# An attention and SwiGLU kernel: the first output tile turned earlier, output products ahead of the last down groups, and other PSUM banks for the first segment's values

## The chip, the cores and the metric

The kernel runs on one core of one Trainium2 chip. The metric is the device time of one execution in microseconds; lower is better. The kernel before has a median of 1744.81 us over three runs (1742.91 to 1745.12).

## The reference

The input x has 2048 rows of D = 576. Two branches are computed from it and mixed row by row with a gate g. Branch a is attention with H = 32 heads of 18 in four segments of 512 rows: softmax inside the segment, and a running memory of the segments before. Branch b is a SwiGLU of width F = 4608. Cut to what matters here:

```python
g = sigmoid((x * gate_w).sum(-1, keepdims=True))
for s in range(4):                                 # segments of 512 rows
    p = softmax(qs @ ks.T * scale + mask)
    o = sig(beta) * (phi(qs) @ M) / (phi(qs) @ z) + (1 - sig(beta)) * (p @ vs)
    M, z = M + phi(ks).T @ vs, z + phi(ks).sum()
a = concat(o) @ wo
b = (silu(x @ w_gate) * (x @ w_up)) @ w_down
out = g * a + (1 - g) * b
```

## The kernel before

The program is one list of instructions, written out by hand in the order in which each engine is to run them; every engine takes its own part of the list strictly in order and waits on semaphores where the data needs it. Products are made exact by splitting both operands into a high and a low part: the high part is made by ScalarE (`split`, L128), the low part by VectorE (L129), and 14 matmuls (`products`, L151) make one product over the 576 rows.

**Projections.** Segment by segment (s = 0 to 3), nine chains make queries and keys (`qk`), then eight value steps (`v_step`, L375) make the values: four blocks of 128 rows for each of two column halves. Every chain and step takes one of TensorE's eight result banks (PSUM) from a cyclic list. Six chains of the first segment use `first_tile`, which cycles through banks 0 to 4 after three chains that hold 0, 1 and 2; so the chains come to stand in banks 0, 1, 2, 3, 4, 0, 1, 2, 3. The value steps take theirs from `v_tile` (L108): 5, 6, 7, 3, 4, 5, 6, 7 in the first segment, then 5, 6, 7 in turn. The next segment's chains use `chain_tile`, banks 0, 1, 2. A bank is free again when ScalarE and VectorE have read the last result out of it. During the first segment's value steps the two engines also split the next segment's x (`x_split`: four tiles xo at L128 and L129, the last one xs at L162 and L163), which the next segment's first chain needs.

**Gate/up units and down groups.** Then 72 units (L1006; two halves of 36, each with its own 1024 rows) make gate and up by seven products apiece (`seven`, L998 and L1001), in three banks: a, y and xx. ScalarE copies and applies silu (L1055 to L1074), VectorE adds and multiplies (L1062 to L1080); the results `sg0` and `sg1` are split into `hh` and `hl` for the down product. After each product a `tick()` runs what `defer(k, ...)` put k ticks ahead. After every third unit 16 down groups are due (`down_group`, L851: nine matmuls over three units, 320 or 256 columns; VectorE adds the result to `ya`, L856), in the next unit's ticks. The attention itself runs in the same ticks. When it is done, `c_open` opens the buffers of the output pass and defers the loads of wo in six chunks (`wo_load`, L888; high part L891, low part L892; chunks 1 to 3 make `wos[0]`, 4 to 6 `wos[1]`) and of the first tiles.

**The output pass** (from L1112) takes 16 tiles of 128 rows. `c_load(n)` fetches a tile of the attention's result (`o`, L897) and, for segments 1 to 3, its memory part (`me`, L901); `f_load(n)` fetches the down result (L908). `c_tr` (L911) adds the two on GpSimd (L913), copies the last 64 columns (L914), turns the tile on TensorE (four matmuls with the identity at L917, one at L919) and splits it (`oh`, `ol`, `os`). One step later the tile is multiplied by `wos[0]` and `wos[1]`, mixed with the gate on VectorE (L1129, L1130) and stored by SyncE (L1133). The last unit leaves 16 down groups behind; the steps of the output pass run them between their own matmuls: `downs(4)` in step 0, `downs(2)` behind each later turn and `downs(1)` behind each half product, as long as there are any. Group 0 is the first that needs hh and hl of the last unit.

Of the kernel before, what the change touches and what calls it, by code (L numbers as in the profile page):

```python
# [65 lines left out]
def gated_mix(ctx, tc, xT, xrest, wf, wfr, wfh, wd, wv, wo, beta, cmask, ident, bmask, out):  # L66
# [32 lines left out]
    def banks(*ids):  # L99
        turn = cycle(ids)  # L100
        return lambda shape=(P, L): ps.tile(list(shape), F32, name=f"bank{next(turn)}")
# [3 lines left out]
    pair_tile = banks(3, 4)  # L105
    first_tile = banks(0, 1, 2, 3, 4)
    lone_tile = banks(7)
    v_tile = banks(5, 6, 7, 3, 4, 5, 6, 7, *8 * (5, 6, 7))  # L108
    a_tile = banks(0)
    x_tile = banks(1)  # L110
    y_tile = banks(2)
# [15 lines left out]
    def split(hi, lo, src):  # L127
        nc.scalar.activation(hi, src, AF.Copy)  # L128
        nc.vector.tensor_sub(lo, src, f32(hi))  # L129
# [31 lines left out]
    def xs_split(xs, raw):  # L161
        nc.scalar.activation(xs, raw, AF.Copy)  # L162
        nc.vector.tensor_sub(xs[64:128], raw[64:128], f32(xs[64:128]))  # L163
# [81 lines left out]
    def r_fetch(f):  # L245
        nc.sync.dma_start(f32(rhs[f % 2][:96]).rearrange("p j n -> p (j n)"), rc[f // 4, :, f % 4])
# [437 lines left out]
    with ExitStack() as st:  # L684
# [12 lines left out]
        def row_tile():  # L697
            return rw.tile([P, L], F32, name="row")

        def w_fetch(f):  # L700
            ops = wops[1, f] = [None] * 7

            def one(j):
                ops[j] = op_tile()
                nc.sync.dma_start(f32(ops[j]).rearrange("p a k n -> p (a k n)"), wc[f, j])

            return [(j + 2 if f else FIRST[j], lambda j=j: one(j)) for j in range(7)]
# [153 lines left out]
        wos, tiles = [], {}  # L861
# [49 lines left out]
        def c_tr(o, me):  # L911
            if me is not None:
                nc.gpsimd.tensor_add(o[:, 0:D], o[:, 0:D], me)  # L913
            nc.gpsimd.tensor_copy(o[:, 576:640], o[:, 512:576])  # L914
            ta = half_tile([P, 4, P])
            for k in range(4):
                nc.tensor.transpose(ta[:, k], o[:, P * k:P * k + P], idt)  # L917
            tb = lone_tile([P, P])
            nc.tensor.transpose(tb, o[:, 512:640], idt)  # L919
            oh = cps[0].tile([P, 4, P], F32R, name="oh")  # L920
            ol = cps[0].tile([P, 4, P], F32R, name="ol")
            os_ = cps[0].tile([P, P], F32R, name="os")
            split(oh, ol, ta)
            xs_split(os_, tb)
            r = []
            for k in range(4):
                r += [oh[:, k], ol[:, k], oh[:, k]]
            return r + [os_, os_]
# [30 lines left out]
        def feed(half, f):  # L959
            return [(f // CH, i, hf, hs, ds, yas[half], half) for i in range(8) for hf in range(2)]  # L960
# [32 lines left out]
        def seven(t, j, first=True):  # L993
# [6 lines left out]
                    n += 1  # L1000
            nc.tensor.matmul(t, rem[:, RPOS[j]], XR[j], start=False, stop=True, skip_group_check=True)  # L1001

        draw = {}
        for o, fn in start:
            defer(o - 7, fn)
        for pos, (half, f) in enumerate(seq):  # L1006
            if f == 0:
                yas[half] = yp.tile([P, 8, D], F32, name="ya")
            q = f % CH
            nxt = seq[pos + 1] if pos + 1 < len(seq) else None  # L1010
            if q == 0 and f:
                groups += feed(half, f - 1)
            plan = []
            if nxt:
                plan += w_fetch(nxt[1]) if nxt[0] and nxt[1] < KEPT else w_make(*nxt)
                if nxt != (0, 1):
                    plan.append((1 if nxt[1] else 10, lambda f=nxt[1]: r_fetch(f)))
                for n, h in enumerate(BLOCKS.get(pos, ())):
                    plan += r_block(h, 4 * n)
                if f + 2 < FT:  # L1020
                    wraw_of[f + 2] = [None, None]
                    for u in range(2):
                        plan.append(((2, 5)[u] if f or not half else 5 + u, lambda u=u, f=f: wraw_of[f + 2].__setitem__(u, w_load(f + 2, u))))
            if pos == FT - 2:
                X2, XR2 = [[None, None] for _ in range(7)], [None] * 7
                plan += [(o + 8, fn) for o, fn in x_second(X2, XR2)]
            for o, fn in plan:
                defer(o + 1, fn)
            step = [0]

            def tick():
                k = step[0]
                step[0] += 1
                if k == 0:
                    while stores:
                        nc.sync.dma_start(*stores.pop(0))
                if half == 0:
                    if (q, k) in ((0, 3), (1, 3), (2, 2)):
                        draw[f] = d_load(f)
                    if (q, k) in ((1, 1), (1, 7), (2, 4)):  # L1040
                        g = f - 1 if k == 1 else f
                        ds[half, g] = d_split(g, draw.pop(g))
                elif (q, k) in ((1, 0), (1, 2), (2, 1)):
                    g = f - 1 if k == 0 else f
                    ds[half, g] = d_fetch(g)
                beat(k, half)

            ops, rem = wops.pop((half, f)), rhs[f % 2]
            hh = fp.tile([P, 2, L], F32R, name="hh")
            hl = fp.tile([P, 2, L], F32R, name="hl")  # L1050
            hs[half, f] = hh, hl
            a, y, xx = a_tile(), y_tile(), x_tile()
            p5, sg0, sg1 = (row_tile() for _ in range(3))
            seven(a, 0)
            nc.scalar.activation(xx, a, AF.Copy)  # L1055
            tick()
            seven(y, 1)
            nc.scalar.activation(p5, y, AF.Copy)
            tick()
            seven(a, 2, False)  # L1060
            y = y_tile()
            nc.vector.tensor_add(y, a, p5)  # L1062
            tick()
            seven(xx, 3, False)
            nc.scalar.activation(sg0, xx, AF.Copy)  # L1065
            tick()
            seven(a, 4, False)
            xx = x_tile()
            nc.scalar.activation(xx, a, AF.Copy)  # L1069
            nc.vector.tensor_add(p5, a, p5)  # L1070
            tick()
            nc.scalar.activation(sg0, sg0, AF.Silu)  # L1072
            seven(y, 5, False)
            nc.scalar.activation(sg1, y, AF.Silu)  # L1074
            exp_table()
            tick()
            tick()
            seven(xx, 6, False)
            nc.vector.tensor_mul(sg0, xx, sg0)
            nc.vector.tensor_mul(sg1, p5, sg1)  # L1080
            if q == CH - 1:
                defer(2, lambda t=(hh[:, 0], hl[:, 0], sg0): split(*t))
            else:
                split_by(2, hh[:, 0], hl[:, 0], sg0)
            split_by(3, hh[:, 1], hl[:, 1], sg1)
            tick()
            assert not groups
            if f == FT - 1:
                groups += feed(half, f)
                if half == 0:  # L1090
                    for n in range(BREAK):
                        beat(None if n > 1 else n)
                    XO, XR = X2, XR2
                    assert not groups
# [13 lines left out]
        def downs(k):  # L1108
            for _ in range(min(k, len(groups))):
                down_group(*groups.pop(0))  # L1110

        ffs = {n: f_load(n) for n in range(2)}  # L1112
        for n in range(17):
            if n < 16:
                if n + 2 < 16:
                    tiles[n + 2] = c_load(n + 2)
                    ffs[n + 2] = f_load(n + 2)
                nxt = c_tr(*tiles.pop(n))
                downs(2 if n else 4)
            if n:  # L1120
                tt = order[n - 1]
                ff = ffs.pop(n - 1)
                for hf in range(2):
                    c = slice(288 * hf, 288 * hf + 288)
                    t = chain_tile()
                    products(t[:, :288], ops, w_mov(wos[hf], 288))
                    downs(1)
                    if hf == 0:
                        nc.vector.tensor_scalar_mul(ff, ff, g1[:, tt:tt + 1])  # L1129
                    nc.vector.scalar_tensor_tensor(ff[:, c], t[:, :288], gg[:, tt:tt + 1], ff[:, c],  # L1130
                                                   op0=OP.mult, op1=OP.add)
                    if hf == 0 and sent:
                        nc.sync.dma_start(*sent.pop(0))  # L1133
                    if n == 16:
                        nc.sync.dma_start(out[0, P * tt:P * tt + P, c], ff[:, c])
                if n < 16:
                    sent.append((out[0, P * tt:P * tt + P, :], ff))
            ops = nxt
# [54 lines left out]
```

## Time and profile before

| | |
|---|---|
| median of three runs | 1744.81 us (1742.91 to 1745.12) |
| the profiled execution | 1747.73 us |
| its span, first to last instruction | 1746.0 us |
| mean granted TensorE clock | 0.998 |
| TensorE busy (matmuls) | 1715.8 us, 98% of the span |
| weight loads, beside the matmuls | 1483.9 us, 85% |
| VectorE, ScalarE, GpSimd busy | 1368.6, 1093.6, 936.3 us |
| DMA queue 1 | 325.83 MB, 76.6% of 16 engines |

A row of the timeline gives the start in us, the time that the piece took, engine, line, operation, output<-input and, in brackets, how long the engine had been idle before it and what ended that. Matmuls overlap, so the spacing of starts tells more than the time of one. PE is TensorE and PEld its weight loads, DVE is VectorE, ACT ScalarE, POOL GpSimd, SPq SyncE's queue of DMA issues.

### The profile page before, as it was taken

The numbers are of one execution on the slowest core, as the hardware profiler recorded it, in microseconds if no ns is written. First come the engines' busy times: TensorE is split into PE (matmuls) and PEld (weight loads), VectorE is DVE, ScalarE is ACT, GpSimd is POOL, SyncE is SP. The second block draws the span as 40 slices with busy tenths as digits, with TensorE's granted clock in tenths as the row PEclk, the third lists the DMA queues.
The fourth block names the chain that finished last, engine by engine and source line by source line (L and its number), as shares of the span: only waits on it lengthen the run. The fifth ranks groups of instructions, "written<-read, shape, count | busy, mean of one in ns | idle before, by whom it ended". The sixth has DMA issues, their size and how long they took to land.

```text
span 1746.0 us, 34931 instructions
## 1 busy us (share of the span) xinstructions
PE 1715.8 (98%) x11868; PEld 1483.9 (85%) x11868; DVE 1368.6 (78%) x3231; ACT 1093.6 (63%) x2198; POOL 936.3 (54%) x1194
## 2 busy tenths in 40 slices
PE   9999999999999999999999999999999999999999
PEld 7899978878888888887887788888888888888799
DVE  6567587989898889898989677787888777887655
ACT  7666575765676577667656755665666576656511
POOL 4434645656665656665666555555555555555221
PEclk9999999999999999999999999999999999999999
DMA  7654499998998888897979976777687668866544
GB/s 263 237 190 154 149 307 179 213 221 180 225 216 206 175 207 199 187 199 192 209 146 287 263 176 132 188 168 157 156 185 173 155 149 186 169 129 147 168 134 139
DMA packets 524003, 328.06 MB, mean 188 GB/s; under 512 B 411184, under 2 KB 460336, under 8 KB 523824
## 3 DMA queue, kind: packets, MB, share of 16 engines
q1 hardware_dynamic: 523824, 325.83, 76.6%
q8 instruction: 93, 1.52, 0.4%
q14 instruction: 86, 0.70, 0.1%
HBM read 165.76 MB, written 76.09 MB: 139 GB/s over the span
## 4 chain that ended last, share of the span: by engine, by line
PE 78%; ACT 8%; DVE 4%; DMA 3%; issue 3%; POOL 2%; SPq 1%; DVEq 0%; ACTq 0%; POOLq 0%
PE bank L998 29%; PE bank L851 25%; PE bank L151 10%; PE bank L1001 5%; PE bank L720 3%; PE bank L768 2%; ACT L1072 1%; PE bank L769 1%; ACT L991 1%; DMA pt<-p 1%; ACT pe L738 1%; PE bank L406 1%; POOL ws L256 1%; DVE hl L941 1%; PE bank L342 1%
## 5 line engine op out<-in xcount | busy, mean ns | idle before, releaser
L753 POOL TENSOR_TENSOR p<-pe,p 128x512 f16<-128x512 f32 x320 | 374.4, 1170 | 457.7 <-DVE p L752 438.2
L851 PE MATMUL bank<-dw,hh 128*128 128x320 f32 (+1 forms) x2304 | 491.2, 306 | 4.1 <-ACT hh L128 2.8
L851 PEld LDWEIGHTS bank<-dw,hh 128*128 128x128 f32 x2304 | 383.3, 191 | 15.6 <-ACT hh L128 3.1
L738 ACT ACTIVATE pe<-bank,mb 128x512 f32<-128x512 f32 (+3 forms) x512 | 246.2, 522 | 219.7 <-DVE mb L726 216.0
L851 PE MATMUL bank<-dw,hl 128*128 128x320 f32 (+1 forms) x1152 | 341.6, 297 | 0.2 <-DVE hl L129 0.2
L726 DVE CUSTOM_DVE_ANT_0 scr<-bank,cm 128x512 bf16<-128x512 f32 (+3 forms) x512 | 246.1, 481 | 7.4 <-PE bank L720 0.6
L851 PEld LDWEIGHTS bank<-dw,hl 128*128 128x128 f32 x1152 | 219.1, 190 | 0.4 <-DVE hl L129 0.4
L856 DVE TENSOR_TENSOR ya<-bank,ya 128x320 f32<-128x320 f32 x352 | 157.7, 452 | 78.7 <-PE bank L851 77.9
L1001 PE MATMUL bank<-xr,rh 128*128 128x512 f32 x504 | 196.3, 390 | 0.0
L746 POOL TENSOR_SCALAR_AFFINE_SELECT pe<-pe 128x256 f32<-128x256 f32 (+1 forms) x320 | 151.1, 473 | 31.2 <-ACT pe L738 21.6
L752 DVE CAST p<-pe 128x512 f16<-128x512 f32 x320 | 145.3, 454 | 2.3 <-DMA pt<-p 2.3
L256 POOL TENSOR_TENSOR ws<-raw 128x256 f32<-128x256 f32 x140 | 123.2, 880 | 15.8 <-DVE wo__22847 L263 4.1
L720 PE MATMUL bank<-kst,qst 108*128 108x512 bf16 (+3 forms) x512 | 125.4, 306 | 5.0 <-ACT pe L738 4.9
L1001 PEld LDWEIGHTS bank<-xr,rh 128*128 128x128 f32 x504 | 94.6, 188 | 20.5
L941 DVE TENSOR_TENSOR hl<-row,hh 128x512 fp32r<-128x512 f32 x120 | 101.4, 845 | 10.8 <-ACT hh L940 10.4
L1065 ACT ACTIVATE row<-bank 128x512 f32<-128x512 f32 x72 | 43.1, 598 | 93.6 <-PE bank L1001 93.5
L1070 DVE TENSOR_TENSOR row<-bank,row 128x512 f32<-128x512 f32 x72 | 49.6, 689 | 58.4 <-ACT bank L1069 58.2
L1072 ACT ACT_TABLE_LOAD x72 | 92.4, 1283 | 1.3
L991 ACT ACT_TABLE_LOAD x72 | 92.4, 1283 | 1.0
L768 PE MATMUL bank<-v,pt 128*128 128x57 bf16 x1280 | 77.0, 188 | 8.8 <-DMA pt<-p 5.7
L1055 ACT ACTIVATE bank<-bank 128x512 f32<-128x512 f32 x72 | 41.7, 579 | 67.0 <-PE bank L1001 66.9
L366 POOL TENSOR_TENSOR q<-qr,q 128x512 bf16<-128x512 f32 x36 | 44.5, 1235 | 72.7 <-ACT q L365 61.9
(2166 smaller groups left out, 4139.0 us busy)
## 6 DMA issues: line engine op xcount, KB each, us to landing
raw<-in_wf_dram SPq DMA_DIRECT2D x140, 256.0 KB
rh<-rc SPq DMA_DIRECT2D x72, 336.0 KB
dc<-dw SPq DMA_DIRECT2D x36, 576.0 KB
dw<-dc SPq DMA_DIRECT2D x36, 576.0 KB
stk<-q SPq DMA_DIRECT2D x32, 384.0 KB
draw<-in_wd_dram SPq DMA_DIRECT2D x36, 288.0 KB
rc<-rt SPq DMA_DIRECT2D x42, 224.0 KB
vd<-vps SPq DMA_DIRECT2D x8, 912.0 KB
```

The lines of the kernel that those rows point to most:

```text
L151: nc.tensor.matmul(t, st[n], mv[n], start=(n == 0), stop=(n == 13))
L256: (nc.gpsimd.tensor_sub if sub else nc.gpsimd.tensor_add)(src[j], p(), q())
L720: nc.tensor.matmul(t[:, c:c + w], qs[:KR, pr, P * i:P * i + P], ks[:KR, pr, 0:w], start=True, stop=True)
L726: nc.vector.tensor_tensor_reduce(scr[:, :w], t[:, c:c + w], cm[:, L - w:L], -SCALE, 3.0e38, OP.add, OP.min, m[:, k:k + 1])
L738: nc.scalar.activation(pe[:, c:c + w], t[:, c:c + w], AF.Exp, bias=m[:, k:k + 1], scale=SCALE)
L746: nc.gpsimd.affine_select(d, d, pattern=pat, compare_op=OP.is_ge, fill=0.0, base=0, channel_multiplier=1)
L752: nc.vector.tensor_copy(p[:, 0], pe)
L753: nc.gpsimd.tensor_sub(p[:, 1], pe, p[:, 0])
L851: nc.tensor.matmul(t, p, q[:, cs], start=(n == 0), stop=(n == 3 * CH - 1))
L856: nc.vector.tensor_add(ya[:, i, cs], t, ya[:, i, cs])
L998: nc.tensor.matmul(t, w[:, p, z], x[z][:, q], start=first and n == 0, stop=False, skip_group_check=True)
L1001: nc.tensor.matmul(t, rem[:, RPOS[j]], XR[j], start=False, stop=True, skip_group_check=True)
```

## The change

Three edits. The fourth and fifth value step of the first segment take banks 4 and 0 instead of 3 and 4. In the last gate/up unit (the one with no next one, `not nxt`) the turn of output tile 0 is deferred to the unit's fourth tick; its result waits in `early`. In the output pass step 0 takes that result and runs no down groups; step 1 runs none behind its turn; all later steps are as before. So the 16 groups last until step 5 instead of step 3.

```diff
-    v_tile = banks(5, 6, 7, 3, 4, 5, 6, 7, *8 * (5, 6, 7))
+    v_tile = banks(5, 6, 7, 4, 0, 5, 6, 7, *8 * (5, 6, 7))
...
+        early = []
         draw = {}
...
             plan = []
+            if not nxt:
+                plan.append((3, lambda: early.append(c_tr(*tiles.pop(0)))))
             if nxt:
...
-                nxt = c_tr(*tiles.pop(n))
-                downs(2 if n else 4)
+                nxt = c_tr(*tiles.pop(n)) if n else early.pop()
+                downs(2 if n > 1 else 0)
```

On TensorE, in the last unit, between its fourth product (bank_22970, tile xx) and its fifth (bank_22968, tile a):

```order
 L998 MATMUL bank_22970<-xo_13174,wo__22957 128x512 x3
 L1001 MATMUL bank_22970<-xr_13044,rh_2332 128x512
+L917 MATMUL bank_23032<-idt,o 128x128 x4
+L919 MATMUL bank_23037<-idt,o 128x128
 L998 MATMUL bank_22968<-xo_13426,wo__22959 128x512 x3
 L998 MATMUL bank_22968<-xo_13268,wo__22959 128x512 x3
```

The five matmuls of tile 0's turn come in here.

On TensorE, behind the last unit's last product, before:

```order
L1001 MATMUL bank_23037<-xr_13177,rh_2332 128x512
L917 MATMUL bank_23081<-idt,o 128x128 x4
L919 MATMUL bank_23086<-idt,o 128x128
L851 MATMUL bank_23095<-dw,hh 128x320 x2
L851 MATMUL bank_23095<-dw,hl 128x320
```

and now (wo_22873 is `wos[0]`):

```order
L1001 MATMUL bank_23053<-xr_13177,rh_2332 128x512
L917 MATMUL bank_23103<-idt,o 128x128 x4
L919 MATMUL bank_23108<-idt,o 128x128
L151 MATMUL bank_23117<-wo_22873,oh 128x288
L151 MATMUL bank_23117<-wo_22873,ol 128x288
```

Before, the turn is that of tile 0 and down group 0 follows. Now it is that of tile 1, and the first half of tile 0's product follows; group 0 comes behind that half, and group 1 behind the second.

On ScalarE, in the same unit, from the copy of the fourth product to the table load for silu, before:

```order
L1065 ACTIVATE row<-bank_22970 128x512
L891 ACTIVATE wo_22874<-raw 128x5x96
L1069 ACTIVATE bank_23037<-bank_22968 128x512
L1072 ACT_TABLE_LOAD
L1072 ACTIVATE row<-row 128x512
```

and now:

```order
L1068 ACTIVATE row<-bank_22970 128x512
L891 ACTIVATE wo_22874<-raw 128x5x96
L128 ACTIVATE oh<-bank_23032 128x512
L162 ACTIVATE os<-bank_23037 128x128
L1072 ACTIVATE bank_23053<-bank_22968 128x512
L1075 ACT_TABLE_LOAD
```

The two high parts of tile 0 stand ahead of the copy that the unit's last product waits for. (From here on the changed kernel's lines are three higher: its L1072 is the L1069 of the kernel before.)

## The prediction

> **What bounds the kernel now.** The sum is made against the profiled execution: its span is 1746.0 us and the execution took 1747.73 us, 2.9 us more than the median of the three runs shown, 1744.81 us (they span 2.2 us). I read the page first, then TensorE's waits over the whole span, since an engine that is busy 98% of it can only be helped where it stands still or runs slowly.
>
> ```profile
> PE 1715.8 (98%) x11868; PEld 1483.9 (85%) x11868; DVE 1368.6 (78%) x3231; ACT 1093.6 (63%) x2198; POOL 936.3 (54%) x1194
> ...
> PE bank L851 <- ACT hh L128: 2.8, 1, 2.8
> ```
>
> The second row's columns are the total, the times and the longest. This is the longest wait that TensorE has anywhere, and it happens once: where the last gate/up unit gives over to the output pass. Two of the three edits are there. TensorE's timeline at the place:
>
> ```profile
> 1644.40 1.52 PE L998 MATMUL bank<-xo,wo__22959 128*128 128x512 f32 x6
> ...
> 1645.98 1.52 PE L998 MATMUL bank<-xo,wo__22983 128*128 128x512 f32 x6
> ...
> 1647.83 1.66 PE L998 MATMUL bank<-xo,wo__22998 128*128 128x512 f32 x6
> ...
> 1649.56 0.60 PE L917 MATMUL bank<-idt,o 128*128 128x128 f32 x4
> ...
> 1653.94 0.56 PE L851 MATMUL bank<-dw,hh 128*128 128x320 f32 x2 [2.80 <-ACT hh L128]
> ...
> 1660.24 0.60 PE L917 MATMUL bank<-idt,o 128*128 128x128 f32 x4
> ...
> 1660.71 0.54 PE L851 MATMUL bank<-dw,hh 128*128 128x320 f32 x2
> ```
>
> The unit's last product (tile xx) begins at 1647.83. Output tile 0 is turned (L917) at 1649.56, down group 0 gets through its six matmuls that need only units 33 and 34, and then TensorE waits 2.80 us for hh of unit 35. From 1660.24 on it works without a gap to the end, so whatever is saved ahead of there is saved from the end. What comes after the wait runs at half speed; in stretches of 3.41 us (busy us of PE first, granted clock after the five engines):
>
> ```profile
> 934.70:938.11 3.41, 1.26 (x15) 1.26 (x16) 2.18 (x5) 3.38 (x7) 0.00 (x0) 1.00 1.00 350
> 938.11:941.53 3.42, 3.42 (x17) 3.42 (x16) 3.16 (x8) 2.65 (x6) 3.27 (x4) 0.50 1.04 404
> 941.53:944.94 3.41, 2.39 (x17) 1.99 (x17) 3.41 (x6) 0.04 (x1) 3.34 (x3) 1.00 1.24 219
> 944.94:948.35 3.41, 3.41 (x27) 3.41 (x26) 3.41 (x6) 1.28 (x2) 3.40 (x3) 1.00 1.06 338
> ...
> 1651.50:1654.91 3.41, 0.80 (x3) 0.55 (x4) 1.65 (x3) 2.96 (x8) 0.06 (x1) 1.00 1.07 391
> 1654.91:1658.33 3.42, 3.17 (x14) 2.87 (x14) 2.58 (x6) 0.14 (x1) 1.65 (x2) 0.50 0.43 160
> ```
>
> A stretch in which TensorE was busy 0.80 us of 3.41 (23%) is followed by one at clock 0.50; so it was at 938, behind 37%; behind 70% the clock stayed full. The half-clock stretch here holds 3.17 us of work and costs half of that, 1.6 us.
>
> **Prices of the work that changes places.**
>
> ```profile
> 1665.21 1.32 PE bank L851 x9
> 1666.54 1.86 PE bank L151 x14
> 1668.39 1.08 PE bank L851 x9
> ```
>
> These are pieces of the chain of waits in order of time: a down group of 320 columns costs 1.32 us, a half of an output product (14 matmuls) 1.86, a group of 256 columns 1.08. A turn costs 0.47 (1660.24 to 1660.71 above), and one of the unit's seven products 1.58 (1644.40 to 1645.98).
>
> **Edit 1, the turn inside the unit.** Five matmuls go ahead of the fifth product at 1644.40: 0.47 us. What they read is there: tile 0's copy on GpSimd ends at 1641.28. The turn is over at 1644.87, long before ScalarE comes to split it. On ScalarE the two splits go behind the fourth chunk of wo (L891) and ahead of L1069, which the unit's last product waits for; on VectorE theirs go ahead of L1070.
>
> ```profile
> 1646.69 0.61 ACT L891 ACTIVATE wo<-raw 128x480 fp32r<-128x480 f32 x1 [1.12 <-DMA raw<-in_wo_dram]
> 1647.20 0.58 ACT L1069 ACTIVATE bank<-bank 128x512 f32<-128x512 f32 x1
> ...
> 1652.76 0.60 ACT L891 ACTIVATE wo<-raw 128x480 fp32r<-128x480 f32 x1 [0.31 <-DMA raw<-in_wo_dram]
> 1653.27 0.61 ACT L128 ACTIVATE hh<-row 128x512 fp32r<-128x512 f32 x1
> ...
> 1654.31 0.57 ACT L128 ACTIVATE oh<-bank 128x512 fp32r<-128x512 f32 x1
> 1654.79 0.27 ACT L162 ACTIVATE os<-bank 128x128 fp32r<-128x128 f32 x1
> 1640.96 0.32 POOL L914 COPY o<-o 128x64 f32<-128x64 f32 x1
> 1649.48 1.44 POOL L913 TENSOR_TENSOR o<-o,me 128x576 f32<-128x576 f32 x1 [8.20 <-DMA me<-med]
> 1650.98 0.58 POOL L914 COPY o<-o 128x64 f32<-128x64 f32 x1
> 1655.89 1.41 POOL L913 TENSOR_TENSOR o<-o,me 128x576 f32<-128x576 f32 x1 [4.33 <-DMA me<-med]
> ```
>
> (ScalarE's rows, then GpSimd's.) oh takes 0.48 to the next start, os about 0.2 (0.27 less the overlap of 0.1 that neighbours show). So L1069 starts at 1647.88 and ends at 1648.46; the last product starts at 1648.5 instead of 1647.83 and ends at 1650.2 instead of 1649.56. Behind it ScalarE's silu chain is 0.7 us later too, but it meets a chunk of wo that lands only at 1652.76 (wait 0.31): 0.1 us is left, and hh is converted at 1653.35 instead of 1653.27.
>
> **Edit 2, products ahead of the groups.** TensorE now meets, in order: the turn of tile 1, the first half of tile 0's product, group 0, the second half, group 1, the turn of tile 2, groups 2 and 3. Each meets its own wait:
>
> ```profile
> 1647.81 0.69 DVE L1070 TENSOR_TENSOR row<-bank,row 128x512 f32<-128x512 f32 x1 [2.20 <-ACT bank L1069]
> 1648.42 1.22 DVE L892 TENSOR_TENSOR wo<-raw,wo 128x480 fp32r<-128x480 f32 x2
> ...
> 1650.43 1.03 DVE L1080 TENSOR_TENSOR row<-row 128x512 f32<-128x512 f32 x1
> ...
> 1653.92 0.69 DVE L129 TENSOR_TENSOR hl<-row,hh 128x512 fp32r<-128x512 f32 x1 [0.77 <-ACT hh L128]
> 1654.53 0.65 DVE L892 TENSOR_TENSOR wo<-raw,wo 128x480 fp32r<-128x480 f32 x1
> ...
> 1655.70 0.68 DVE L129 TENSOR_TENSOR ol<-bank,oh 128x512 fp32r<-128x512 f32 x1
> 1656.41 0.29 DVE L163 TENSOR_TENSOR os<-bank,os 64x128 fp32r<-64x128 f32 x1
> ```
>
> Tile 1's sum on GpSimd waits for a DMA until 1649.48 and ends at 1650.92, the copy at 1651.56: the turn runs from 1650.95 to 1651.6, with some 0.75 us of idling ahead of it. The first half needs wo's third chunk (VectorE, below): 1651.6 to 1653.5. Group 0's six early matmuls, two thirds of 1.32, to 1654.35; hh is there at 1653.35 + 0.61 = 1653.96, hl 0.1 later than now, at 1654.70; the group ends at 1654.85. The second half needs the low part of the last wo chunk, VectorE's 1654.53 row, 0.1 later: 1655.28; two of its matmuls go before, the rest ends at 1656.9. Group 1 to 1657.95. Tile 2's sum ends at 1655.89 + 1.41 = 1657.30, so its turn does not wait: 1658.4. Groups 2 and 3: 1660.8.
>
> Now the kernel has group 3 and the turn of tile 0 behind it at 1660.24, and would need two turns and a whole product more for the same work: 1660.24 + 0.47 + 3.72 + 0.47 = 1664.9. The gain is 4.1 us. That is nearly all of the stall of 2.80 and the half clock's 1.6.
>
> The last groups move from output step 3 to step 5. I cost that at nothing: TensorE does the same work there, and the cover for VectorE's evictions, the loads and the stores is TensorE's own time, since it waits for none of them from 1660.24 on, in steps with groups or without. SyncE's list is the same; only tile 4's loads, held until the turn of tile 1 is done, go about 7 us earlier, into a busy stretch (DMA share 1.07 above), behind tile 2's. Holding tile 2 up by 1 us would cost 0.4 (it has 0.65 to spare): 0 to 0.4, and I take 0, since they are issued last.
>
> One price is open. On VectorE, ol and os (0.72 and 0.32 from start to start, 1655.70 and 1656.41) start when oh ends, at 1647.80, and go ahead of L1070, which moves from 1647.81 to 1648.84; the third wo chunk (L892) follows 0.61 later, at 1649.45; tile 1's sum starts on GpSimd at 1649.48. Operations of these two that both read SBUF stand in each other's way: GpSimd's copy beside the 1650.43 product (1.03 us) took 0.58 us, the one at 1640.96 took 0.32. If GpSimd is first, VectorE is late but catches up before 1653.92, because ScalarE is later still: 0. If VectorE is first, the sum ends 0.6 later, and 0.65 reaches the end; behind both chunks it would be 1.1. It is a tie, and I take 0.2, nearer to the first, as the sum then starts at its DMA's time: 3.9 us.
>
> [...]
>
> **Edit 3, the first segment's values.** The fourth value step takes bank 4 instead of 3, the fifth 0 instead of 4.
>
> ```profile
> 43.72 1.85 PE L151 MATMUL bank<-vw,xo 128*128 128x288 f32 x12 [1.26 <-DVE ph L368]
> ...
> 56.04 0.19 PEld L151 LDWEIGHTS bank<-xs,qhi 128*128 128x128 f32 x1 [0.34 <-DVE xs L163]
> ...
> 54.53 0.61 ACT L162 ACTIVATE xs<-xo 128x512 fp32r<-128x512 f32 x1
> ...
> 55.17 0.82 DVE L163 TENSOR_TENSOR xs<-xo,xs 64x512 fp32r<-64x512 f32 x1 [0.60 <-ACT xs L162]
> ```
>
> (TensorE and its loads, ScalarE, then VectorE.) The 1.26 us go: bank 3 is held by the last key chain, banks 4 and 0 by chains that ended four and three earlier. But the next thing that TensorE meets is the next segment's first chain, whose last two matmuls need xs, split by ScalarE at 54.53 and VectorE until 55.99; today it waits for that at 56.04. Those two engines have been taking turns with the evictions and wait for each other, not for TensorE (0.60 us in the 55.17 row, ended by ScalarE). So TensorE comes up to 1.3 us earlier, waits that much longer for xs (or, on the way, for the fifth step's evictions, since the chain now takes its bank 0), and goes on at 56.04 as now. Bounds: a gain of 1.3 if something in that chain did hang on TensorE, a loss of 0.2 for another restart; I take 0.
>
> **Rivals.** [...] The worst 3.41 us after the change hold 0.45 us of idling at the last product (the fifth and sixth end at 1644.40 + 0.47 + 2 × 1.58 = 1648.03, it starts at 1648.5) and 0.9 around the turn: busy 60%, between 37% (throttled) and 70% (not), nearer to the second, so I take no throttling; with it 1.6 is lost. A variant: the two half-clock stretches start 716.80 us apart, 210 times 3.413, so they look like windows of a fixed grid, and how it falls on the stall is a matter of phase. With an edge in the middle of the 2.80 us both windows are over half busy, the kernel before is not slowed either, and 4.1 becomes 2.5; the runs' spread of 2.2 us allows it.
>
> [...]
>
> *Edit 3 pays as well* (1.3 more: 1739.6). For: the wait does go. Against: the xs rows.
>
> *Slower: the last chunk of wo.* TensorE takes its list in order, and the second half of product 0 comes to stand ahead of groups 1 to 15, and starts 2.5 us behind the chunk's landing at 1652.76; in the kernel before, that half starts at 1666.54, 11 us behind the chunk's readiness. Each us by which that chunk lands later is a us on the end: from 1656.9 on nothing is gained, at 1660.4 the kernel is 0.2% slower (1748.3). For: it crosses the busiest stretch, share 1.07. Against: nothing is put ahead of it in its queue.
>
> **How the numbers follow.** Forecast (stall filled, edit 3 nothing): 1744.81 − 3.9 = 1740.9 us, chance 0.52; the wait moves 0.28; edit 3 pays 0.14; slower 0.06. 0.2% of the median is 3.5 us, about what a measurement of this kernel tells from no change. Three quarters of the forecast's cases gain more than that, all of edit 3's, and a few of the second's: faster 0.55, same 0.39, slower 0.06. The range: 1738.4 is a gain of 5.4 with 1 us of the runs' spread; 1744.0 is a gain of 1.4 less 0.6 of it.
>
> **What would show it.** Right: no TensorE wait on hh over 0.3 us at the seam; an idle of 0.7 to 0.9 us ahead of the turn of tile 1, ended by GpSimd, and 0.2 to 0.5 at the last product and the second half; full clock from 1645 to the end; group 3 ending near 1660.8 on the old time scale; no wait at the fourth value step, 0.7 to 1.8 us in all at the first chain of the next segment, and its last two matmuls starting at 56.04 as now. Wrong: a clock of 0.50 behind the seam, TensorE waiting over 1.5 us for GpSimd or over 1 us for wo, or the next segment's chains starting a us earlier.

## The result, and the profile after

| | before | after |
|---|---|---|
| median | 1744.71 us (22 runs, 1742.30 to 1747.66) | 1741.30 us (22 runs, 1739.23 to 1746.13) |
| ratio | | 0.9981, 95% interval 0.9975 to 0.9988 |
| profiled execution | 1747.73 us | 1742.64 us |
| its span | 1746.0 us | 1740.9 us |
| mean granted clock | 0.998 | 0.999 |

The change is worth 3.4 us, 0.2%. First, from the waits of TensorE over the whole span of the changed kernel (total, times, longest), the longest single one and the rows that the change touches:

```profile
PE bank L851 <- DVE ya L856: 2.9, 1, 2.9
...
PE bank L151 <- ACT vps L391: 0.7, 1, 0.7
PE bank L151 <- DVE xs L163: 0.6, 1, 0.6
PE bank L851 <- ACT hh L128: 0.5, 2, 0.3
```

The wait for hh, 2.8 us in one piece before, is down to 0.5 in two pieces, of which 0.30 is at the seam (the other is in the middle of the kernel). The two L151 rows are edit 3's place, see below. The first row is a wait for VectorE's addition into `ya` in the middle of the kernel, and not the change's doing: it is 2.9 us in the first profile of edit 3 alone too, which has the old seam. In the profile of before it is 1.02 us, and there a stretch at half clock (938.11 to 941.53 us, clock 0.50) lies ahead of it:

```profile
943.80 0.51 PE L851 MATMUL bank<-dw,hh 128*128 128x256 f32 x2 [1.02 <-DVE ya L856]
```

TensorE's timeline at the seam, changed kernel:

```profile
1643.45 0.39 PE L1001 MATMUL bank<-xr,rh 128*128 128x512 f32 x1
1643.68 0.60 PE L917 MATMUL bank<-idt,o 128*128 128x128 f32 x4
...
1647.44 1.62 PE L998 MATMUL bank<-xo,wo__22998 128*128 128x512 f32 x6
...
1649.12 0.60 PE L917 MATMUL bank<-idt,o 128*128 128x128 f32 x4
...
1649.58 0.38 PE L151 MATMUL bank<-wo,oh 128*128 128x288 f32 x1
...
1652.87 0.56 PE L851 MATMUL bank<-dw,hh 128*128 128x320 f32 x2 [0.30 <-ACT hh L128]
...
1653.59 0.41 PE L851 MATMUL bank<-dw,hl 128*128 128x320 f32 x1 [0.17 <-DVE hl L129]
...
1656.92 0.60 PE L917 MATMUL bank<-idt,o 128*128 128x128 f32 x4
...
1659.99 0.30 PE L151 MATMUL bank<-wo,oh 128*128 128x288 f32 x1
```

Tile 0's turn takes 0.46 us inside the unit. Behind the last product come the turn of tile 1 (1649.12) and the first half product (1649.58), with no idle time; TensorE idles 0.30 us for hh and 0.17 for hl; tile 2's turn starts at 1656.92, and the last groups of this piece are over at 1659.99, where the next product begins. Counted in steps of 3.41 us from the stretch at clock 0.50 that this profile has at 815.17 to 818.58 (the clock's grid, below), the two stretches that hold those waits and what follows:

```profile
1651.44:1654.85 3.41, 2.94 (x18) 2.29 (x18) 2.66 (x4) 2.54 (x6) 1.25 (x1) 1.00 1.06 392
1654.85:1658.26 3.41, 3.41 (x28) 3.37 (x27) 3.31 (x6) 0.64 (x2) 3.02 (x5) 1.00 0.92 342
```

The emptiest of the seam holds 2.94 us of work (86%), against 0.80 before, and the clock stays at 1.00.

**One yardstick for all runs.** The rows on xr and rh end the unit's products. The one ahead of the fifth product starts at 1643.45 here (first row above); before it is this one:

```profile
1644.17 0.39 PE L1001 MATMUL bank<-xr,rh 128*128 128x512 f32 x1
```

From there to the end of the span every kernel has the same work to do (the fillers of one experiment apart), so the *rest* = span less that start compares the seams and nothing else: 1746.0 − 1644.17 = 101.8 us before, 1740.9 − 1643.45 = 97.5 after. Of the 5.1 us between the two spans, 4.4 were gained there. The other 0.7 (1644.17 − 1643.45) lie ahead of the yardstick row, and do not belong to the change: the first value step, which nothing of the change precedes, already starts 2.3 us earlier, and part of that was lost again on the way (the wait of 2.85 us in the middle is part of it). Before:

```profile
36.73 1.74 PE L151 MATMUL bank<-vw,xo 128*128 128x288 f32 x12
```

and after, followed by the two waits of the table above:

```profile
34.46 1.74 PE L151 MATMUL bank<-vw,xo 128*128 128x288 f32 x12
...
50.30 0.70 PE L151 MATMUL bank<-xo,qhi 128*128 128x512 f32 x2 [0.70 <-ACT vps L391]
...
53.82 0.50 PE L151 MATMUL bank<-xs,qhi 128*128 128x512 f32 x1 [0.55 <-DVE xs L163]
```

From the first value step to the matmul on xs it is 56.04 − 36.73 = 19.3 us before and 53.82 − 34.46 = 19.4 after. The wait of 1.26 us at the fourth step is gone, and 0.70 + 0.55 = 1.25 have come in its place, for the first bank (0) of the next segment's chain and for xs.

### The profile page after: what moved, and what is told of

Its sections match the earlier page's. It is cut to its first block, busy times and chain, and to the rows that moved or that the text cites. A ratio compares the mean times of both kernels' runs of the same rounds, so it can differ in the third digit from the quotient of the medians.

```text
span 1740.9 us, 34931 instructions
## 1 busy us (share of the span) xinstructions
PE 1713.9 (98%) x11868; PEld 1481.7 (85%) x11868; DVE 1371.2 (79%) x3231; ACT 1093.9 (63%) x2198; POOL 937.4 (54%) x1194
## 4 chain that ended last, share of the span: by engine, by line
PE 76%; ACT 8%; DVE 5%; issue 4%; DMA 3%; POOL 3%; SPq 1%; DVEq 0%; POOLq 0%; ACTq 0%
PE bank L998 29%; PE bank L851 24%; PE bank L151 10%; PE bank L1001 5%; PE bank L720 3%; PE bank L768 2%; DMA pt<-p 2%; ACT L1075 1%; PE bank L769 1%; ACT L991 1%; PE bank L406 1%; POOL ws L256 1%; ACT pe L738 1%; PE bank L452 1%; PE bank L342 1%
## 5 line engine op out<-in xcount | busy, mean ns | idle before, releaser
L941 DVE TENSOR_TENSOR hl<-row,hh 128x512 fp32r<-128x512 f32 x120 | 102.1, 851 | 10.7 <-ACT hh L940 10.2
L151 PE MATMUL bank<-xo,qhi 128*128 128x512 f32 x264 | 83.1, 396 | 0.7 <-ACT vps L391 0.7
```

Of the source, the lines that this page charges most:

```text
L151: nc.tensor.matmul(t, st[n], mv[n], start=(n == 0), stop=(n == 13))
```

## The experiments

Eight runs in two groups of four, each group with its own runs of the kernel before: a median of 1745.01 us over 33 runs with a mean granted clock of 0.9973 for edit 3 alone, edits 1 and 2 alone and the two halves of the seam's edit, and 1745.06 us over 31 runs with 0.9976 for the other four.

| run | median us | ratio (95%) | mean granted clock of its runs | rest after the yardstick in its profile, us | clock 0.50 behind the seam, us |
|---|---|---|---|---|---|
| before (first profile) | | | | 101.8 | 3.41 |
| changed (first profile) | | | | 97.5 | none |
| edit 3 alone | 1743.20 | 0.9990 (0.9981 to 0.9999) | 0.9982 | 102.3 | 6.83 |
| edit 3 alone, again | 1744.63 | 1.0000 (0.9992 to 1.0008) | 0.9978 | 100.1 | none |
| edits 1 and 2 alone | 1740.69 | 0.9976 (0.9967 to 0.9985) | 0.9986 | 97.4 | none |
| early turn, old group places | 1744.68 | 0.9997 (0.9988 to 1.0005) | 0.9970 | 102.1 | 6.83 |
| new group places, late turn | 1747.06 | 1.0015 (1.0006 to 1.0024) | 0.9965 | 104.1 | 6.83 |
| before, with fillers in the stall | 1743.57 | 0.9989 (0.9980 to 0.9997) | 0.9985 | 100.4 | none |
| changed, last wo chunk later | 1743.99 | 0.9992 (0.9984 to 1.0001) | 0.9977 | 99.9 | none |
| changed, again | 1740.44 | 0.9971 (0.9960 to 0.9982) | 0.9987 | 97.8 | none |

**Edit 3 alone.**

```diff
-    v_tile = banks(5, 6, 7, 3, 4, 5, 6, 7, *8 * (5, 6, 7))
+    v_tile = banks(5, 6, 7, 4, 0, 5, 6, 7, *8 * (5, 6, 7))
```

> The kernel before with edit 3 alone (the first segment's fourth and fifth value step in banks 4 and 0). Theory (the first segment's end is set by ScalarE and VectorE taking turns): no change, ratio 0.9997 to 1.0003; the last two matmuls of the next segment's first chain, which wait for xs, start 19.3 us behind the first value step as before (56.04 - 36.73), and TensorE's wait of 1.26 us at the fourth step is gone and comes back ahead of them. Rival (edit 3 pays for itself): 1.3 us less, ratio 0.9993, and those matmuls start 18.0 us behind the first value step.

The first comparison ended just below 1, so it was made once more:

> Edit 3 alone once more, since the first comparison ended with an interval that just left 1 out. Theory (the 1.26 us wait for the bank is only moved to the wait for xs): ratio 0.9995 to 1.0003; a lower ratio would come with a higher mean granted clock over its runs than the kernel before has, and at equal clock the two would agree within 0.5 us. Rival (edit 3 pays its 1.26 us): 0.9990 to 0.9994 with the same mean clock in both kernels.

The second gave 1.0000. The two profiles of this one kernel explain why they could differ: they are not alike at a place that the edit does not touch. The seam in the first, by the clock's grid:

```profile
1646.76:1650.18 3.42, 1.09 (x7) 0.69 (x5) 2.40 (x5) 3.15 (x7) 0.19 (x1) 1.00 1.07 382
1650.18:1653.59 3.41, 3.17 (x13) 2.76 (x13) 3.22 (x7) 0.68 (x3) 1.65 (x2) 0.50 0.88 328
1653.59:1657.00 3.41, 3.41 (x16) 3.41 (x15) 0.49 (x1) 0.00 (x0) 1.65 (x2) 0.50 0.01 6
```

and in the second:

```profile
1645.60:1649.02 3.42, 2.08 (x14) 1.65 (x13) 3.24 (x4) 3.39 (x7) 1.64 (x2) 1.00 1.13 334
1649.02:1652.43 3.41, 2.04 (x12) 1.58 (x12) 2.99 (x7) 1.72 (x5) 0.96 (x1) 1.00 1.05 391
1652.43:1655.84 3.41, 2.87 (x22) 2.88 (x23) 1.48 (x4) 0.00 (x0) 2.35 (x4) 1.00 0.22 81
```

In the first the stall for hh fell into one window, busy for 1.09 us (32%), and two windows at half clock followed. In the second an edge of the grid cut the stall into two windows that were busy for 2.08 and 2.04 us (60%), and the clock stayed full. The rest is 102.3 us in the one and 100.1 in the other: 2.2 us between two executions of one kernel. The stall itself differs by 0.4 us of that (2.33 for hh in the first). At full clock (1.00 in the rows above) another wait shows; TensorE's timeline of the second:

```profile
1649.62 0.55 PE L851 MATMUL bank<-dw,hh 128*128 128x320 f32 x2 [1.94 <-ACT hh L128]
...
1652.97 0.56 PE L851 MATMUL bank<-dw,hh 128*128 128x320 f32 x2 [1.13 <-DVE ya L856]
```

Behind the 1.94 us for hh come 1.13 us for VectorE's addition into `ya`, a wait of 0.26 us in the first profile of the kernel before, whose row (1654.91 to 1658.33) has clock 0.50. For edit 3 itself, look at where the next segment's first matmul on xs starts: 18.4 to 19.4 us behind the first value step in the seven profiles with the new banks, 18.3, 19.1 and 19.3 in those with the old ones. The means, 18.8 and 18.9, differ by 0.1 us, so no gain of 1.3 us is in these; and the wait that edit 3 removes is 1.26, 1.01 and 0.24 us in the three with the old banks, so the 1.26 was one draw. In the mean over the runs the kernel was 1.5 us below the kernel before in the first comparison, and even with it (1744.95 against 1744.93) in the second. The first comparison came with a higher mean clock (0.9982 against 0.9973), as the expectation for the second had said it would; at the hardware section's 0.9 us for each 0.001 of clock that accounts for some 0.8 of the 1.5 us, and the rest is left without a cause. The times of the two comparisons together neither show a gain nor exclude a small one.

**Edits 1 and 2 alone** (the two later edits of the change, with the old list of banks).

> The changed kernel with the old banks, so edits 1 and 2 alone. Theory (the filled stall is all of the gain): 3.0 to 4.2 us less than before, ratio 0.9976 to 0.9983, as the whole change; no half clock at the seam. Rival (edit 3 carries a part): a gain of 2.1 to 2.6 us, ratio 0.9985 to 0.9988.

It measured 0.9976, no less than the whole change (0.9981 and, below, 0.9971): there is no sign that edit 3 carries a part. With intervals of some 1.6 us to either side these runs alone could not show one of 1.3 us; the profiles above can.

**The two halves of the seam's edit, one at a time.** Early turn, but step 0 runs four groups as before:

```diff
-                downs(2 if n > 1 else 0)
+                downs(2 if n else 4)
```

(against the changed kernel)

> The changed kernel with the down groups in their old places (four in step 0, two behind each later turn): the turn of tile 0 is in the unit, but products do not go ahead of groups. Theory: the turn only gives TensorE something to do earlier; it then stands still that much longer for hh. Wait for hh 2.9 to 3.5 us, half clock behind it as before, time within 0.5 us of before (ratio 0.9997 to 1.0003). Rival (the turn inside the unit is itself worth its 0.47 us, or costs the 0.7 us by which it holds up the unit's last product): ratio 0.9997 or 1.0004 and the wait for hh unchanged at 2.8.

New places of the groups without the early turn:

```diff
-    v_tile = banks(5, 6, 7, 3, 4, 5, 6, 7, *8 * (5, 6, 7))
+    v_tile = banks(5, 6, 7, 4, 0, 5, 6, 7, *8 * (5, 6, 7))
...
-                downs(2 if n else 4)
+                downs(2 if n > 1 else 0)
```

(against the kernel before)

> The changed kernel without the turn in the unit: tile 0 is turned at the seam, its product follows the turn of tile 1, ahead of the groups. Theory: the product needs ol and os of tile 0, which VectorE makes behind hh, hl and the last wo chunk (1655.70 to 1656.70 in the trace of before), so TensorE stands still for 4 to 5 us, the half clock stays, and the kernel is 0.5 to 3 us slower than before, ratio 1.0003 to 1.0017. Rival (the order alone fills the stall): a gain of 1 us or more, ratio below 0.9995.

Neither pays. With the early turn alone the wait for hh is about what it was:

```profile
1650.24 0.90 PE L851 MATMUL bank<-dw,hh 128*128 128x320 f32 x2 [2.66 <-ACT hh L128]
```

The 2.9 to 3.5 us of the theory did not come; the time is as it expected, and half clock followed (0.50 for 6.83 us from 1649.81). With the order alone TensorE waits twice as long; its timeline:

```profile
1645.12 0.27 PE L919 MATMUL bank<-idt,o 128*128 128x128 f32 x1
1645.23 0.60 PE L917 MATMUL bank<-idt,o 128*128 128x128 f32 x4
1651.32 0.45 PE L919 MATMUL bank<-idt,o 128*128 128x128 f32 x1 [5.50 <-DVE os L163]
```

Tile 0's turn ends at 1645.2, tile 1's follows at once, and its last matmul needs the bank out of which VectorE still has to split `os` of tile 0. On ScalarE tile 0's split now stands behind the unit's silu work, two chunks of wo and hh (its oh starts at 1648.78), on VectorE its os only at 1650.88, so TensorE stands for 5.50 us (4 to 5 were expected). The early turn gets tile 0's split out of the way before the two engines turn to the unit's last results. Without it the kernel is 0.15% slower than before.

**The half clock by itself.** The kernel before, with eleven matmuls that nobody reads in the stall:

```diff
+                    if n == 6 and cps and i == 0 and hf == 0 and c == FT // CH - 1:
+                        warm = ps.tile([P, L], F32, name="bank6")
+                        for _ in range(11):
+                            nc.tensor.matmul(warm, cm[:, 0:P], cm, start=True, stop=True)
```

> The kernel before with edit 3's bank list left as it was, and eleven matmuls of 128 x 512 that write a free bank and that nobody reads, put on TensorE into the idle time behind the last product matmul of group 0 that does not need hh (some 11 x 0.21 = 2.4 us of the 2.80 us stall). Theory (the half-clock window is the stall's second price): the stall's length stays, TensorE still leaves it when hh has been written, but no window at half clock follows it, and groups 1 to 3 run at 0.21 us a matmul: 0.8 to 1.6 us less than the kernel before (ratio 0.9991 to 0.9995), since the kernel before does not fall to half clock there equally in every run. Rival (the gain is the filled stall alone, the clock takes no part): ratio 1.0000, and a window at half clock behind the stall all the same.

TensorE's timeline of this kernel:

```profile
1649.33 2.55 PE L856 MATMUL bank<-cm 128*128 128x512 bf16 x11
1651.62 0.56 PE L851 MATMUL bank<-dw,hh 128*128 128x320 f32 x2
```

The fillers take 2.3 us of the stall (0.21 apiece, 1649.33 to 1651.62), and the first matmul on hh starts where it would without them: 8.8 us behind the yardstick row (9.8 in the first profile of before, 8.5 in the second of edit 3 alone). (The 0.21 us a matmul that the expectation gives the groups is the spacing at half clock, 0.63 for three of 256 columns from 1654.92 in the profile of before; behind the fillers it was 0.12, 0.35 for three from 1652.60.) The kernel gained 1.5 us of median (0.9989, the interval ending at 0.9997; 0.8 to 1.6 us was expected), with the mean clock of its runs at 0.9985 against 0.9976 for the kernel before in the same group. In this profile itself the fillers bought nothing: its rest of 100.4 us is about that of the second profile of edit 3 alone (100.1), where the grid had cut the stall in two. That they pay in the executions in which it does not is how gain and clock fit together, but no profile shows it, and this is one comparison: the first of edit 3 alone gave as much (0.9990) and did not repeat.

**The last chunk of wo later** (changed kernel; its load goes behind those of tiles 0 to 2 instead of into the unit's ninth step, its conversion behind hh):

```diff
-            for n, (hf, z) in zip((1, 2, 4, 5, 8, 9), ((0, 0), (0, 1), (0, 2), (1, 0), (1, 1), (1, 2))):
+            for n, (hf, z) in zip((1, 2, 4, 5, 8), ((0, 0), (0, 1), (0, 2), (1, 0), (1, 1))):
...
                 if n == 0:
+                    wo_load(1, 1, slice(192, 288))
+                    while due:
+                        for fn in due.popleft():
+                            fn()
```

> The changed kernel, with the last chunk of the output weights not loaded in the ninth step of the last unit but behind the loads of tile 0 and tile 1, so that it lands about 4 us later and is converted behind hh. Theory (the order of the changed kernel lives on that chunk's being there): TensorE stops for 3 to 4.5 us at the second half of the first output product, which needs the chunk, and the gain of the seam goes: 3 to 5 us more than the changed kernel, ratio to the kernel before 0.9993 to 1.0010, and if a half-clock window follows the new stall up to 1.0015. Rival (the chunk has slack of that size, the products of the first half and group 0 cover it): as the changed kernel, 0.998.

In this kernel's timeline, TensorE, then ScalarE, VectorE and GpSimd:

```profile
1647.87 0.66 PE L917 MATMUL bank<-idt,o 128*128 128x128 f32 x4 [0.89 <-POOL o L913]
...
1653.85 0.40 PE L151 MATMUL bank<-wo,oh 128*128 128x288 f32 x1 [1.86 <-ACT wo L891]
1653.19 0.60 ACT L891 ACTIVATE wo<-raw 128x480 fp32r<-128x480 f32 x1 [2.84 <-DMA raw<-in_wo_dram]
1645.90 2.44 DVE L892 TENSOR_TENSOR wo<-raw,wo 128x480 fp32r<-128x480 f32 x2
1646.25 1.57 POOL L913 TENSOR_TENSOR o<-o,me 128x576 f32<-128x576 f32 x1 [7.77 <-DMA me<-med]
```

The second half product waits 1.86 us for the chunk, less than the 3 to 4.5 expected: hh now goes ahead of a conversion and is no longer waited for, which gives back a part. The rest is 99.9 us, 2.1 to 2.5 more than the changed kernel's two profiles have (97.5, 97.8), and the median 3.5 us more than that of the changed kernel in the same group. The mean clock of its runs is lower too (0.9977 against 0.9987), while its one profile has no slow window at the seam. The chunk is on the path, as the theory and the prediction's slower rival had it; the median price is within the 3 to 5 us expected.

**The changed kernel again.**

> The changed kernel as it stands, on the same chip as the three others. Theory: 0.9975 to 0.9985, no half-clock window at the seam, mean granted clock about 0.001 above that of the kernel before. Rival (its gain was that chip's): a ratio above 0.9990.

0.9971, in seven runs. With the first comparison (0.9981) and edits 1 and 2 alone (0.9976), three comparisons of this seam agree within their intervals.

## Why the prediction was right, step by step

The forecast was the filled stall with 3.9 us of gain; 3.4 was measured in the first comparison and 4.6 in the second. The gain of 1.4 us behind the upper end of its range was the author's estimate, and no run shows it: in both profiles of the changed kernel the turn of tile 1 follows the last product without a wait. Edit 3 did not pay, and the slower case did not come.

Counted from the yardstick row, the predicted path of TensorE and the measured one:

| | predicted, us | measured, us | second profile, us |
|---|---|---|---|
| last product starts | 4.3 | 4.0 | 4.3 |
| turn of tile 1 | 6.8 | 5.7 | 6.0 |
| first half product | 7.4 | 6.1 | 6.5 |
| first matmul on hh | 10.2 | 9.4 | 9.7 |
| last of group 3 ends | 16.6 | 16.5 | 16.9 |
| the same work in the kernel before | 20.7 | | |

Its end, and so the gain of the seam (4.1 predicted; 20.7 − 16.5 = 4.2, and 3.8 in the second profile), came out right.

**Edit 1** cost 0.46 us, as priced. That the last product would then wait for ScalarE was priced too high: the fourth chunk of wo landed 0.36 us earlier against the yardstick than in the profile of before, and the weight loads waited 0.24 us. That is one draw again: in the second profile they waited 0.53 us, and the product started where it was predicted.

**The turn of tile 1 was to wait 0.75 us for GpSimd; it did not.** The step took the landing of that tile's `me` from one execution. Its sum started 5.3 us behind the yardstick there. In the changed kernel (GpSimd's row, then others of its timeline that are used next):

```profile
1647.16 1.44 POOL L913 TENSOR_TENSOR o<-o,me 128x576 f32<-128x576 f32 x1 [6.58 <-DMA me<-med]
...
1653.60 1.79 POOL L913 TENSOR_TENSOR o<-o,me 128x576 f32<-128x576 f32 x1 [4.39 <-DMA me<-med]
1651.21 1.08 ACT L891 ACTIVATE wo<-raw 128x480 fp32r<-128x480 f32 x2
1652.20 0.61 ACT L128 ACTIVATE hh<-row 128x512 fp32r<-128x512 f32 x1
1654.02 1.92 DVE L941 TENSOR_TENSOR hl<-row,hh 128x512 fp32r<-128x512 f32 x1
```

it started 3.7 us behind it, and in the other profiles between 3.8 and 5.0, with the load issued at the same place. The profile of before happened to show the latest. Where it came late again (5.0, the run with the later chunk), TensorE did wait for GpSimd: the 0.89 us in its timeline above. The idle time lay in the path all the same, only elsewhere: ScalarE converts two chunks of wo (1651.21), then hh, and TensorE, there earlier, waits 0.30 for that. The prediction had no wait there: it had hh ready at 1653.96, 0.4 us before TensorE would come to it (1654.35). By the spacing of starts group 0 took 2.3 us (1651.52 to 1653.84) instead of the 1.35 that the sum gives it. What sets the pace there is ScalarE's list, not TensorE's, as the sum had it; that the two come within 0.1 to 0.3 us of each other at the end is partly luck.

**VectorE beside GpSimd.** The delay was feared at one place and came at another: the split `hl` at 1654.02 took 1.92 us instead of 0.69, beside GpSimd's sum of 1653.60, which took 1.79 instead of 1.44. No wait of TensorE follows from it. The feared place showed it in the run with the later chunk (and, 2.41 us, in the one with the late turn): two L892 took 2.44 us (1.22 in the kernel before) beside the sum of 1646.25, which took 1.57; the 0.89 us that the turn behind it waited came mostly from `me`, not from these 0.13. So the 0.2 us stood for a cost that came to 0 in the changed kernel's first profile. What the rows show of the two is this: with `hl` at 1654.02, GpSimd's sum ends at 1655.39, and 0.55 us later `hl` ends. Not every such pair was slowed: in the profile of before GpSimd's copy at 1728.15 took 0.24 us and VectorE's L1129 beside it (1728.18) 0.52, as both do with nothing beside them.

**Half clock.** That the change removes the slow window was right, and so was the prediction's variant of a moving phase. The forecast's 4.1 us is about what this change gains over an execution with one slow window (101.83 − 97.45 = 4.4); over one with none it gains 100.1 − 97.6 = 2.5 (97.6 is the mean of the three profiles with the seam's edits), the very 2.5 us of that variant; over one with two, 102.3 − 97.6 = 4.7. A median over executions mixes the three, and the 3.4 to 4.6 us measured lie between the ends. That the profile to which the sum was made had one slow window, and not none or two, was luck: the same sum would have come to 2.5 or 4.7. That the clock has its part is shown by the profiles, two executions of one kernel above all; the fillers point the same way. How often each case comes was not counted, since only one execution of each kernel has a profile, but the mean clocks give an estimate: 0.9987 with the change against 0.9976 without is 0.0011 of 1745 us, 1.9 us or about one window an execution. The grain of the forecast, 0.1 us, was finer than this allows.

**The share of work behind which the clock stayed up** was placed between 37% and 70%: 60% was taken as safe. The rows bear that out: the windows busy 60% and 61% (2.04 and 2.08 us; edit 3 alone, again) were followed by clock 1.00, those busy 23%, 32% and 35% (0.80 us before, 1.09 with edit 3 alone, 1.18 with the early turn alone) by 0.50. Over the rest of the profile of the changed kernel, in the same steps, the nearest on either side are 1.62 us (811.76 to 815.17, 48%), followed by 0.50, and 1.78 and 1.81 us (from 941.46 and 292.93, 52% and 53%), followed by 1.00; what lies between was not shown there. A stall of 2.33 us that fell into one window was followed by half clock (edit 3 alone), one of 1.94 across an edge was not (the same kernel again).

**Edit 3** showed no gain, for the reason given: the 1.26 us came back as 0.70 + 0.55 at the next segment's chain, on the two reads that the prediction had named, xs and the bank's evictions.

**The slower rival** had the right mechanism. By its rule a load issued 3.8 us later costs 3.8 us; the profiles show 2.1 to 2.5, since the wait for hh goes, and the medians 3.5, in which the clock has a part.

## What to carry to other kernels

Fill a stall with work whose operands are ready, and make them ready first: the order alone lost 0.15%, the early turn alone gained nothing, together they gained 0.2 to 0.3%. A wait removed ahead of another engine's chain (ScalarE's and VectorE's splits here) is only moved; look at what the next consumer waits for. Behind one and the same seam there were 6.83 us at half clock in one execution (stall 2.33 us) and none in another (1.94), so a single profile of a seam shows one draw.

## What the runs showed of the hardware

**The clock's grid moves.** In the profile of before the stretches at clock 0.50 last 3.41 us each (from 938.11 and from 1654.91) and start 716.80 us apart, 210 times 3.413; in that of the changed kernel one starts at 815.17 and the last at 1740.18, 271 times 3.413 apart. Counted from the first instruction, the steps of 3.413 us on which they lie begin at 2.86 and 2.80 us in these two, and at 1.54, 1.17 and 0.61 us with edit 3 alone, the early turn alone and the late turn (slow from 1650.18, 1649.81 and 1649.25). So the phase differs from run to run, and the seam of the kernel before had 0, 3.41 or 6.83 us at half clock behind the same stall (0 and 6.83 in the two profiles of edit 3 alone). What makes it one window or two was not found: in the profile of before the clock came back after a slow window with 3.17 us of work, with edit 3 alone it stayed low after a window with the same 3.17. Over 64 runs of the kernel before, the time follows the mean granted clock: 1746.6 us at 0.996 (9 runs), 1745.5 at 0.997 (28), 1744.4 at 0.998 (16), 1743.8 at 0.999 (10), 1741.6 at 1.000 (1). That is some 0.9 us for each 0.001. One window at half clock, by estimate half of its 3.41 us and so 1.7 of 1745, is 0.001 of the mean; by the same estimate it costs less than 1.7 where a wait is the shorter for it, as that for `ya` was: 0.26 us behind it, 1.13 at full clock.

**The start differs by 2 us.** In two-microsecond windows of the kernel before

```profile
4.00:6.00 2.00, 0.86 (x3) 0.00 (x0) 0.00 (x0) 0.53 (x1) 0.00 (x0) 1.00 0.93 276
6.00:8.00 2.00, 1.85 (x4) 1.49 (x5) 1.81 (x5) 1.87 (x8) 0.00 (x0) 1.00 1.05 351
```

and of the changed one, whose program is the same up to there:

```profile
4.00:6.00 2.00, 2.00 (x6) 0.98 (x4) 1.19 (x4) 1.23 (x4) 0.00 (x0) 1.00 0.87 245
6.00:8.00 2.00, 2.00 (x10) 1.63 (x9) 0.67 (x2) 1.33 (x5) 0.00 (x0) 1.00 1.04 349
```

TensorE idles for 1.1 us in the one and not in the other, and then gets through 4 instructions instead of 10. The first value step starts at 36.73 in this profile and between 34.3 and 35.4 in the nine others. A comparison of two profiles from their start would have credited edit 3 with these 2.3 us.
